# A sparse-attention and gelu kernel: the lead-in of batch 0 and the value rows of batch 1 rearranged

## The chip, the core and the metric

The kernel runs on one core of one Trainium2 chip. The metric is the device time of one execution in microseconds, as the median of several runs.

## What is computed

The input is q, k and v (4 batches, 8 heads, 768 positions, 64 numbers each, float32) and two matrices. Each position attends to its neighbours closer than 16 and, besides, to 24 block keys and block values: the maximum of the keys, and the mean of the values, over blocks of 32. The result goes through two matrix products with a gate between.

```
k_sum = k.reshape(B, H, nb, block, D).max(axis=3)      # block = 32, nb = 24
v_sum = v.reshape(B, H, nb, block, D).mean(axis=3)
scores_l = scale * q @ k^T, kept where |i - j| < 16
scores_s = scale * q @ k_sum^T + log(32)
a = softmax(concat(scores_l, scores_s)); attn = a @ concat(v, v_sum)
x = attn as (3072, 512); h = x @ w_in                  # (512, 2048)
out = (h * sigmoid(1.702 * h)) @ w_out                 # (2048, 512)
```

## The kernel before

The program is one long list of instructions for five engines: TensorE (PE in the profile), VectorE (DVE), ScalarE (ACT), GpSimd (POOL) and SyncE (SP). A small wrapper, `_Ordered`, keeps every instruction in the order in which it is written, so each engine works through its own part of that list in order and waits where an operand isn't ready. All instructions carry line 28, that of the wrapper; the profile's groups are therefore told apart by tile names.

The work goes by batches of 768 positions. Batch 0 is done in two units of 384 positions, unit 0 and unit 1 of the code's `ff_out(u, ...)`: the first half of batch 0, then its second half. Batches 1 to 3 are done whole, with a product in seven parts (`product`) instead of the plain one. For each unit there is an input stage (`ff_in` or `ff_open`: `ph` tiles in PSUM, 128 x 384, four matmuls each, a gelu by ScalarE into `gT`) and an output stage (`ff_out`, twelve slots of four matmuls into `po`). The attention for the next unit is laid between the slots of the output stage by the tables `plan0`, `plan1` and `plan`, and the turning of its keys and queries between the groups of the input stage by the table `todo`. In these tables `s` are scores with an exp by ScalarE, `m` a mask by VectorE, `v` values (`ps_av`, then VectorE's reciprocal and product into `x`), `x` the turning of `x` into `xT`, `t` the turning of queries (`tq`), `R` the value rows (`value_rows`), `g` an early load of the gelu table.

The lead-in is the attention of the first half of batch 0, before any input matmul can run. `load_k0` brings the keys as float32 into `kraw` by DMAs that SP and ScalarE issue; `k_cast` casts them on VectorE into `kb`; `k_turn` turns them on TensorE (`ps_k`), `k_own` copies them into `kn` (shown as `qT`), `k_max` makes the block keys (`ks`), `k_blocks` copies these into `ksz`. Queries, values, `w_in`, the second half's queries and `w_out` come by DMAs that GpSimd issues, which cast on the way. `s_own`, `s_edges` and `b_turn` make the scores to own rows, neighbouring rows and block keys; `v_sum` the block sums of the values (`ps_vt`); `av_own`, `av_edges` and `av_blocks` the values; `v_norm`, `x_turn` and `x_copy` lead to `xT`; `ff_first` is the beginning of the input stage. The mask of the own rows, `near`, and of the edges, `edge`, are added by matmuls with the identity. GpSimd builds them (`masks0`) from tiles that VectorE has filled; the masks of the later stages, `mk`, come from GpSimd in `finish_masks`, which stands ahead of the `w_out` loads.

After the lead-in come, on GpSimd, a copy of rows inside `vw`, the block sums into `vs` (`vrows0`) and the loads of batch 1 (`load_batch(1)`: keys, queries, values); on SP the halo rows (`vw<-vw`) and the sum rows (`vw<-vs`), which the values of unit 0's output stage read.

`value_rows(1)`, the same for batch 1, sums 32 values on TensorE (`vsum`, `ps_vs`), adds on VectorE (`vpart`, `vs`), and lets SP copy the sums into `vw`. It stands in slot 1 of unit 1's output stage; the values that read these rows stand in slot 6.

PSUM is held by two pools for the whole kernel: `pmm`, four tiles of one bank, and `psb`, two tiles of two banks.

Of the kernel before, what the change touches and what calls it, by code (L numbers as in the profile page):

```python
# [35 lines left out]
def kernel(  # L36
# [38 lines left out]
    psb = ctx.enter_context(tc.tile_pool(name="psb", bufs=2, space=bass.MemoryType.PSUM))  # L75
    pmm = ctx.enter_context(tc.tile_pool(name="pmm", bufs=4, space=bass.MemoryType.PSUM))


# [3 lines left out]
    kraw = lead.tile([128, NP, 2, 2, JH * D], F32, name="kraw")  # L82
    kb2, qb2 = {}, {}

    def load_k0(p):
        for e in range(2):
            (act if e else sp).dma_start(out=kraw[:, p, e], in_=k[0, 2 * p:2 * p + 2, e * HALF:(e + 1) * HALF]
                          .rearrange("h (p r) d -> p h (r d)", r=JH))

    def load_q0(half):  # L90
        t = qb2["half", half] = castp2.tile([128, H, JH, D], BF16, name="qb", tag="qb")
        for g in range(2):
            pool.dma_start(out=t[:, 4 * g:4 * g + 4].rearrange("p h r d -> p h (r d)"),
                           in_=q[0, 4 * g:4 * g + 4, half * HALF:(half + 1) * HALF]
                           .rearrange("h (p r) d -> p h (r d)", r=JH))
# [32 lines left out]
    ident = consts.tile([128, 128], BF16, name="ident")  # L128
    E = consts.tile([128, 20 + 128], BF16, name="E")
    warm = lead.tile([128, 512], BF16, name="warm")  # L130
    near = lead.tile([128, JH, 128], BF16, name="near")
    edge = lead.tile([128, NP * JH, 32], BF16, name="edge")
    dve.memset(warm, 0.0)
    dve.memset(E, 0.0)
    sub = E[:, 20:148].rearrange("p (g c) -> p g c", c=block)[:, :, 0:4]
    dve.memset(sub, 1.0)
    dve.memset(near, 0.0)
    dve.memset(edge, FAR)
    dve.memset(edge[0:32], 0.0)
    dve.memset(edge[96:128], 0.0)  # L140
# [5 lines left out]
    def bias(ap, base, pattern, cp):  # L146
        pool.affine_select(out=ap, in_=ap, compare_op=ALU.is_ge, fill=FAR,
                           base=base, pattern=pattern, channel_multiplier=cp)

    def selectors():  # L150
        pool.affine_select(out=sub, in_=sub, compare_op=ALU.is_ge, fill=0.0, base=0,
                           pattern=[[0, 4], [-block, 4]], channel_multiplier=1)
        pool.affine_select(out=sub, in_=sub, compare_op=ALU.is_ge, fill=0.0, base=block - 1,
                           pattern=[[0, 4], [block, 4]], channel_multiplier=-1)

    def masks0():
        reach = window - 1
        bias(near, reach, [[0, JH], [-1, 128]], 1)
        bias(near, reach, [[0, JH], [1, 128]], -1)
        n = NP * JH  # L160
        bias(edge[0:32], reach - 32, [[0, n], [1, 32]], -1)
        bias(edge[96:128], reach - 32, [[0, n], [-1, 32]], 1)
# [32 lines left out]
    ks0 = [keep.tile([128, nb], BF16, name=f"ks0{p}") for p in range(NP)]  # L195
    ksz = lead.tile([128, NP, 64], BF16, name="ksz")
# [15 lines left out]
    def clear_values(eng, s):  # L212
        eng.memset(vw[s][96:128, 0], 0.0)
        eng.memset(vw[s][32:64, NQ - 1], 0.0)
        eng.memset(vw[s][:, :, :, D:VC], 1.0)

    def clear_sums(eng):

        eng.memset(ksz, 0.0)
        eng.memset(vs, 0.0)  # L220
        eng.memset(vs4, 0.0)
# [3 lines left out]
        eng.memset(vs[:, :, D:VC], float(block))  # L225
# [32 lines left out]
    def vsum(s):  # L258

        ps = vs_ps[0] = [pmm.tile([128, 512], F32, name="ps_vs", tag="mm") for e in range(2)]  # L260
# [10 lines left out]
    def warmth(n):  # L271

        for i in range(n):
            ps = pmm.tile([128, 512], F32, name="ps_w", tag="mm")
            pe.matmul(out=ps, lhsT=warm[:, 0:128], rhs=warm, start=True, stop=True)

    def busy(n):
        ps = pmm.tile([128, 512], F32, name="ps_w", tag="mm")
        for i in range(n):
            pe.matmul(out=ps[:, 0:128], lhsT=warm[:, 0:128], rhs=warm[:, 0:128],  # L280
                      start=True, stop=True)
# [87 lines left out]
    def k_cast(p, eng):  # L369
        if p % 2 == 0:  # L370
            kb2[p // 2] = castp2.tile([128, 2, 4, JH, D], BF16, name="kb", tag="kb")
        copy(eng, runs_of(kb2, p).rearrange("p e h r d -> p e h (r d)"), kraw[:, p])

# [7 lines left out]
    def k_turn(p):  # L381
        ps = st["K", p] = pmm.tile([128, 1024], BF16, name="ps_k", tag="mm")
        for e in range(2):
            turn_plain(ps[:, e * HALF:e * HALF + HALF], runs_of(kb2, p)[:, e])
# [5 lines left out]
    def k_max(p):  # L390
        dve.tensor_reduce(out=ks0[p], in_=kn[:, p].rearrange("p (n s) -> p n s", s=block),
                          axis=AX.X, op=ALU.max)

    def k_blocks(p, eng):

        eng.tensor_copy(out=ksz[0:64, p, 0:nb], in_=ks0[p][0:64])
        eng.tensor_copy(out=ksz[64:128, p, 32:32 + nb], in_=ks0[p][64:128])
# [8 lines left out]
    def q_turn(p, half):  # L406
        st["Q", p] = pmm.tile([128, 1024], BF16, name="ps_q", tag="mm")
        turn_plain(st["Q", p][:, 0:HALF], qb2["half", half][:, 2 * p:2 * p + 2])
# [647 lines left out]
```

## Time and profile before

| | |
|---|---|
| median of 3 runs | 229.48 us (228.01 to 229.67) |
| the profiled execution | 229.11 us, of which the span of the profile is 227.1 us |
| TensorE matmul | busy 208.5 us, 92% of the span |
| TensorE weight load | busy 138.4 us, 61% |
| VectorE, ScalarE, GpSimd | busy 132.1, 123.2 and 88.2 us |
| mean granted clock of TensorE | 0.977 |
| software DMA queue (GpSimd) | 12.85 MB, 61456 packets |
| hardware DMA queues | 14.52 and 0.79 MB |
| read from HBM, written | 27.26 and 6.29 MB |

The page divides the span into 40 slices of 5.7 us and gives for each engine a digit, its busy share in tenths; `PEclk` is the clock that TensorE was granted, in tenths. Other answers give busy times for chosen stretches, the waits with what ended them, and the instructions in order of time: start, busy time, engine, operation, out<-in, how many were merged, and in brackets the idle time before with its releaser. "Issue to landing" of a DMA counts from the issue instruction to the arrival of the data. "Start" is in microseconds from the start of the span.

### The profile page before, as it was taken

The numbers are of one execution on the slowest core, as the hardware profiler recorded it, in microseconds if no ns is written. First come the engines' busy times: TensorE is split into PE (matmuls) and PEld (weight loads), VectorE is DVE, ScalarE is ACT, GpSimd is POOL, SyncE is SP. The second block draws the span as 40 slices with busy tenths as digits, with TensorE's granted clock in tenths as the row PEclk, the third lists the DMA queues.
The fourth block names the chain that finished last, engine by engine and source line by source line (L and its number), as shares of the span: only waits on it lengthen the run. The fifth ranks groups of instructions, "written<-read, shape, count | busy, mean of one in ns | idle before, by whom it ended". The sixth has DMA issues, their size and how long they took to land.

```text
span 227.1 us, 5821 instructions
## 1 busy us (share of the span) xinstructions
PE 208.5 (92%) x2354; PEld 138.4 (61%) x2354; DVE 132.1 (58%) x388; ACT 123.2 (54%) x232; POOL 88.2 (39%) x150
## 2 busy tenths in 40 slices
PE   6288899999999869899999999998999999999992
PEld 1245666455555335466578886664788866668882
DVE  6867752559466356479866571698665715543211
ACT  2255478446656614377676354775763547773220
POOL 7998971663359988069448400000000000000000
PEclk9769999999999969999999999999999999999999
DMA  6999999999509999999999957792311680000222
GB/s 190 205 147 196 200 215 219 192 164 189 84 0 92 163 144 151 134 141 148 141 151 156 144 108 213 137 180 38 74 46 49 84 226 16 3 0 0 95 92 94
DMA packets 89146, 28.52 MB, mean 126 GB/s; under 512 B 76816, under 2 KB 86048, under 8 KB 89120
## 3 DMA queue, kind: packets, MB, share of 16 engines
q0 software_dynamic: 61456, 12.85, 68.7%
q1 hardware_dynamic: 26576, 14.52, 29.5%
q10 hardware_dynamic: 1088, 0.79, 1.1%
q8 instruction: 18, 0.29, 0.6%
q14 instruction: 8, 0.07, 0.1%
HBM read 27.26 MB, written 6.29 MB: 148 GB/s over the span
## 4 chain that ended last, share of the span: by engine, by line
PE 65%; DVE 21%; issue 5%; DMA 4%; ACT 2%; SPq 1%; DVEq 0%; ACTq 0%
PE ph L28 23%; PE poA L28 14%; PE po L28 6%; DVE gs L28 6%; PE poB L28 6%; DVE ks L28 4%; PE ps_av L28 4%; PE poC L28 3%; PE ps_s L28 3%; DMA kx<-kb 2%; DVE kx L28 2%; DVE qT L28 2%; PE ps_q L28 2%; DVE x L28 1%; PE ps_t L28 1%
## 5 line engine op out<-in xcount | busy, mean ns | idle before, releaser
L28 PE MATMUL ph<-xT,w_in_sb 128*128 128x384 bf16 x512 | 86.3, 326 | 1.8 <-DVE vpart L28 0.9
L28 ACT ACTIVATE gT<-ph 128x384 f16<-128x384 f32 x128 | 61.4, 491 | 29.7 <-PE ph L28 29.7
L28 PEld LDWEIGHTS <-w_in_sb 128*128 128x128 bf16 x512 | 49.4, 98 | 35.7 <-issue 4.0
L28 PEld LDWEIGHTS <-gT 128*128 128x128 f16 x312 | 29.3, 98 | 11.9 <-issue 0.9
L28 POOL DMA_DIRECT2D vw<-in_v_dram x44 | 31.2, 734 | 10.4 <-DMA vw<-in_v_dram 2.6
L28 DVE TENSOR_TENSOR gs<-gT 128x384 f16<-128x384 f16 x48 | 17.1, 355 | 26.7 <-ACT gT L28 26.6
L28 ACT ACTIVATE a_sb<-ps_s 128x768 bf16<-128x768 f32 x32 | 24.6, 806 | 13.4 <-PE ps_s L28 13.4
L28 PEld LDWEIGHTS <-gs 128*128 128x128 f16 x288 | 27.5, 98 | 3.9 <-issue 0.4
L28 PE MATMUL po<-w_out_sb,gT 128*128 128x512 f16 x96 | 23.9, 390 | 0.0
L28 POOL DMA_DIRECT2D qb<-in_q_dram x24 | 19.3, 832 | 7.9 <-DMA w_out_sb<-in_moe_w_out_dram 3.5
L28 POOL DMA_DIRECT2D kb<-in_k_dram x20 | 16.3, 843 | 8.7 <-DMA kx<-kb 8.6
L28 PE MATMUL poA<-ws,gs 128*128 128x256 f16 x144 | 18.7, 273 | 0.1
L28 DVE TENSOR_TENSOR x<-ps_av,rc 128x384 bf16<-128x384 f32 x32 | 17.8, 558 | 1.1
L28 DVE TENSOR_TENSOR a_sb<-a_sb,mk 128x768 bf16<-128x768 bf16 x28 | 14.6, 553 | 2.6 <-ACT a_sb L28 2.3
L28 ACT ACTIVATE s<-poA 128x256 f32<-128x256 f32 x14 | 5.4, 386 | 18.6 <-PE poA L28 18.3
L28 ACT ACT_TABLE_LOAD x10 | 12.8, 1283 | 3.1 <-issue 2.9
L28 DVE RECIPROCAL rc<-ps_av 128x6 f32<-128x6 f32 x32 | 6.0, 187 | 12.3 <-PE ps_av L28 12.3
L28 DVE TENSOR_TENSOR osb<-poC,s 128x256 f32<-128x256 f32 x9 | 3.8, 421 | 15.9 <-PE poC L28 14.2
L28 PE MATMUL ps_av<-vw,a_sb 128*64 128x65 bf16 (+1 forms) x360 | 9.0, 203 | 2.2 <-DMA vw<-vs 2.2
L28 PEld LDWEIGHTS <-a_sb 128*64 128x64 bf16 (+1 forms) x360 | 7.5, 116 | 5.3 <-issue 4.0
L28 ACT ACTIVATE osb<-po 128x512 f32<-128x512 f32 x6 | 3.6, 598 | 11.8 <-issue 6.2
L28 PEld LDWEIGHTS <-kx 64*128 64x128 bf16 x336 | 6.0, 95 | 5.5 <-issue 3.9
(90 smaller groups left out, 230.0 us busy)
## 6 DMA issues: line engine op xcount, KB each, us to landing
out_dram<-osb SPq DMA_DIRECT2D x24, 256.0 KB, 2.5
vw<-in_v_dram POOLq DMA_DIRECT2D x36, 64.0 KB, 5.9
w_out_sb<-in_moe_w_out_dram POOLq DMA_DIRECT2D x4, 512.0 KB, 12.7
qb<-in_q_dram POOLq DMA_DIRECT2D x8, 192.0 KB, 10.0
w_in_sb<-in_moe_w_in_dram POOLq DMA_DIRECT2D x3, 512.0 KB, 9.8
kb<-in_k_dram POOLq DMA_DIRECT2D x16, 96.0 KB, 5.5
qb<-in_q_dram POOLq DMA_DIRECT2D x16, 96.0 KB, 4.3
vw<-vs SPq DMA_DIRECT2D x6, 198.0 KB, 5.5
```

The lines of the kernel that those rows point to most:

```text
L28: r = f(*a, **kw)
```

## The change

The change has these parts.

- Keys of batch 0: GpSimd issues their loads too, in three DMAs that cast to bfloat16, mixed with the first queries. `kraw` and `k_cast` are gone.
- VectorE's memsets: `clear_keys`, most of `clear_values` and those of `vs` stand after the lead-in.
- Masks: `near` and `edge` are made by VectorE from the identity, by a row of running maxima (`bands`); one edge mask serves all heads. GpSimd makes the identity only. The selector `E` is made by memsets.
- On GpSimd the `w_out` loads stand ahead of `finish_masks`.
- PSUM: the lead-in has three pools of its own (`pidle`, `pturn`, `pbig`), which are closed at its end; `pmm` and `psb` open after it.
- TensorE: ten wide filler matmuls at the start instead of eight, and thirty narrow ones between the first steps (`idle`). The lead-in's order is new: edge scores in two groups, block scores straight from `ks0` by eight matmuls of 32 columns, block sums by matmuls of 32 columns into one tile that a matmul with zeros clears first, copied by one instruction.
- Batch 1: in unit 1's input stage the turns follow each other group by group, all four query turns are there, by `turn_both` with one copy each, and `value_rows(1)` stands behind group 13. In the output stage `plan1` is spread anew; the values of batch 1 draw from `pmm`, the sums (`vsum`) of all batches from `psb`. The last turn of `x` lies between the first input matmuls of batch 1.

```diff
     outp = ctx.enter_context(tc.tile_pool(name="outp", bufs=3))
-    psb = ctx.enter_context(tc.tile_pool(name="psb", bufs=2, space=bass.MemoryType.PSUM))
-    pmm = ctx.enter_context(tc.tile_pool(name="pmm", bufs=4, space=bass.MemoryType.PSUM))
-
-
+    first = ExitStack()
+    pidle = first.enter_context(tc.tile_pool(name="pidle", bufs=2, space=bass.MemoryType.PSUM))
+    pturn = first.enter_context(tc.tile_pool(name="pturn", bufs=2, space=bass.MemoryType.PSUM))
+    pbig = first.enter_context(tc.tile_pool(name="pbig", bufs=2, space=bass.MemoryType.PSUM))
 
     early = ExitStack()
...
-    kraw = lead.tile([128, NP, 2, 2, JH * D], F32, name="kraw")
-    def load_k0(p):
-        for e in range(2):
-            (act if e else sp).dma_start(out=kraw[:, p, e], in_=k[0, 2 * p:2 * p + 2, e * HALF:(e + 1) * HALF]
-                          .rearrange("h (p r) d -> p h (r d)", r=JH))
-
-    def load_q0(half):
-        t = qb2["half", half] = castp2.tile([128, H, JH, D], BF16, name="qb", tag="qb")
-        for g in range(2):
+    def load_k0(p0, p1):
+        for p in range(p0, p1, 2):
+            if p % 2 == 0:
+                kb2[p // 2] = castp2.tile([128, 4, 2, JH, D], BF16, name="kb", tag="kb")
+        o = 2 * (p0 % 2)
+        n = 2 * (p1 - p0)
+        pool.dma_start(out=kb2[p0 // 2][:, o:o + n].rearrange("p h e r d -> p (h e) (r d)"),
+                       in_=k[0, 2 * p0:2 * p1].rearrange("h (e p r) d -> p (h e) (r d)", e=2, r=JH))
+
+    def load_q0(half, gs_):
+        if 0 in gs_:
+            qb2["half", half] = castp2.tile([128, H, JH, D], BF16, name="qb", tag="qb")
+        t = qb2["half", half]
+        for g in gs_:
             pool.dma_start(out=t[:, 4 * g:4 * g + 4].rearrange("p h r d -> p h (r d)"),
...
+    def identity():
+        pool.memset(wide, 0.0)
+        pool.affine_select(out=ident, in_=ident, compare_op=ALU.not_equal, fill=1.0,
+                           base=0, pattern=[[-1, 128]], channel_multiplier=1)
...
-    def masks0():
-        reach = window - 1
-        bias(near, reach, [[0, JH], [-1, 128]], 1)
-        bias(near, reach, [[0, JH], [1, 128]], -1)
-        n = NP * JH
-        bias(edge[0:32], reach - 32, [[0, n], [1, 32]], -1)
-        bias(edge[96:128], reach - 32, [[0, n], [-1, 32]], 1)
+        dve.memset(E, 0.0)
+        for g in range(4):
+            dve.memset(E[32 * g:32 * g + 32, 20 + g:21 + g], 1.0)
+
+    def bands():
+
+        n = 128 + 2 * PAD
+        src, step = wide, 1
+        for dst in (band[0], band[1], band[0], band[1]):
+            n -= step
+            dve.tensor_tensor(out=dst[:, 0:n], in0=src[:, 0:n], in1=src[:, step:step + n], op=ALU.max)
+            src, step = dst, 2 * step
+        n -= 15
+        dve.tensor_tensor(out=band[0][:, 0:n], in0=band[1][:, 0:n], in1=band[1][:, 15:15 + n], op=ALU.max)
+        dve.tensor_scalar(out=band[1][:, 1:1 + n], in0=band[0][:, 0:n], scalar1=-FAR, scalar2=FAR,
+                          op0=ALU.mult, op1=ALU.add)
+        dve.memset(edge, FAR)
+        dve.tensor_copy(out=edge[0:32], in_=band[1][0:32, 2:34])
+        dve.tensor_copy(out=edge[96:128], in_=band[1][96:128, 162:194])
...
     def clear_values(eng, s):
         eng.memset(vw[s][96:128, 0], 0.0)
-        eng.memset(vw[s][32:64, NQ - 1], 0.0)
-        eng.memset(vw[s][:, :, :, D:VC], 1.0)
+        eng.memset(vw[s][96:128, 0, :, D:VC], 1.0)
+        if s:
+            eng.memset(vw[s][32:64, NQ - 1], 0.0)
...
     def vsum(s):
 
-        ps = vs_ps[0] = [pmm.tile([128, 512], F32, name="ps_vs", tag="mm") for e in range(2)]
+        big = psb.tile([128, 1024], F32, name="ps_vs", tag="big")
+        ps = vs_ps[0] = [big[:, 0:512], big[:, 512:1024]]
...
-    def warmth(n):
+    def idle(n, cols=128):
...
+            pe.matmul(out=st["H", 0][:, 0:cols], lhsT=warm[:, 0:128], rhs=warm[:, 0:cols],
                       start=True, stop=True)
...
-    def k_cast(p, eng):
-        if p % 2 == 0:
-            kb2[p // 2] = castp2.tile([128, 2, 4, JH, D], BF16, name="kb", tag="kb")
-        copy(eng, runs_of(kb2, p).rearrange("p e h r d -> p e h (r d)"), kraw[:, p])
...
-    def b_turn(p):
-
-        if p % 2 == 0:
-            st["B", p // 2] = pmm.tile([128, 512], F32, name="ps_b", tag="mm")
-        r = slice(p % 2 * 64, p % 2 * 64 + 64)
-        pe.matmul(out=st["B", p // 2][r, 0:HALF], lhsT=ksz[:, p, :],
-                  rhs=qT[p][0][:, 0:HALF], start=True, stop=True)
+    def e_exp(g):
+        for h in range(2):
+            if g == 0:
+                st["ah", h] = lead.tile([128, HALF], BF16, name="ah", tag=f"ah{h}")
+            o = slice(g * EG, g * EG + EG)
+            act.activation(out=st["ah", h][:, o], in_=st["H", h][:, o], func=ACT.Exp, scale=scale)
+
+    def b_turn(g):
+
+        st["B", g] = pturn.tile([128, 512], F32, name="ps_b", tag="turn")
+        for i in range(2):
+            for h in range(2):
+                o = i * 64 + h * 32
+                r = slice(h * 64, h * 64 + 64)
+                pe.matmul(out=st["B", g][o:o + 32, 0:HALF], lhsT=ks0[r, 2 * g + i],
+                          rhs=qT[2 * g + i][0][r, 0:HALF], start=True, stop=True, skip_group_check=True)
...
-    def v_sum(p):
-
-        if p == 0:
-            st["VT"] = pmm.tile([128, 512], F32, name="ps_vt", tag="mm")
-        r = slice(p % 2 * 64, p % 2 * 64 + 64)
-        for j in range(NJ):
-            o = 20 - 4 * j
-            pe.matmul(out=st["VT"][r, p * 128:p * 128 + 128], lhsT=E[:, o:o + 64],
-                      rhs=vw[0][:, 2 * j + 1, 2 * p:2 * p + 2, 0:D],
-                      start=(j == 0), stop=(j == NJ - 1), skip_group_check=True)
-
-    def v_copy(p, *engs):
-        for hh in range(2):
-            r0 = p % 2 * 64 + hh * 32
-            o = p * 128 + hh * D
-            copy(engs[hh], vs4[r0:r0 + nb, 2 * p + hh, 0:D], st["VT"][r0:r0 + nb, o:o + D])
+    def v_sum(ps_):
+
+        n = len(ps_) * 2 * D
+        p0 = ps_[0]
+        ps = st["VT"] = pturn.tile([128, 512], F32, name="ps_vt", tag="turn")
+        pe.matmul(out=ps[:, 0:n], lhsT=warm[:, 0:128], rhs=warm[:, 0:n], start=True, stop=False,
+                  skip_group_check=True)
+        for p in ps_:
+            for i in range(2):
+                r0, c0 = (p % 2 * 2 + i) * 32, ((p - p0) * 2 + i) * D
+                for j in range(NJ):
+                    o = 20 - 4 * j
+                    pe.matmul(out=ps[r0:r0 + 32, c0:c0 + D], lhsT=E[:, o:o + 32],
+                              rhs=vw[0][:, 2 * j + 1, 2 * p + i, 0:D],
+                              start=False, stop=(j == NJ - 1), skip_group_check=True)
+
+    def v_copy(ps_, eng):
+        n = 2 * len(ps_)
+        copy(eng, vs4[:, 2 * ps_[0]:2 * ps_[0] + n, 0:D],
+             st["VT"][:, 0:n * D].rearrange("p (h d) -> p h d", d=D))
 
...
     def tq(p, s, eng):
-        for half in range(2):
-            ps = pmm.tile([128, 512], F32, name="ps_q", tag="mm")
-            turn_runs(ps[:, 0:HALF], runs_of(qb2, p)[:, half])
-            copy(eng, qT[p][s][:, half * HALF:half * HALF + HALF], ps[:, 0:HALF])
+        ps = turn_both(runs_of(qb2, p))
+        copy(eng, qT[p][s].rearrange("p (e x) -> p e x", e=2), ps)
...
     def values(b, half, g):
 
-        ps = psb.tile([128, 1024], F32, name="ps_av", tag="big")
+        if b == 1:
+            banks = [pmm.tile([128, 512], F32, name="ps_av", tag="mm") for i in range(2)]
+        else:
+            ps = psb.tile([128, 1024], F32, name="ps_av", tag="big")
+            banks = [ps[:, i * 512:i * 512 + 512] for i in range(2)]
...
-    def ff_open(nts):
+    def ff_open(nts, between):
 
         phs = {nt: pmm.tile([128, HALF], F32, name="ph", tag="mm") for nt in nts}
         for kos in ((0, 1), (2, 3)):
             for nt in nts:
                 ff_step(phs[nt], 0, nt, kos)
+            if between and kos[0] == 0:
+                between()
         for nt in nts:
...
-    for p in range(NP):
-        load_k0(p)
+    dve.memset(warm, 0.0)
+    load_k0(0, 1)
     exp_soon()
-    clear_values(dve, 0)
-    clear_sums(dve)
-    for s in range(2):
-        clear_keys(dve, s)
-    clear_values(dve, 1)
-    make_identity(nc, ident)
-    masks0()
-    selectors()
-    load_q0(0)
+    identity()
+    load_k0(1, 2)
+    load_q0(0, (0,))
+    load_k0(2, 4)
+    load_q0(0, (1,))
     for h in range(H):
         load_v0(h)
     for n0, n1 in ((0, 256), (256, 512), (512, 1024), (1024, 1536), (1536, 2048)):
         load_w_in(n0, n1)
     w50 = vw[0].rearrange("p (j e) h c -> p j e h c", e=2)
-    load_q0(1)
-    finish_masks()
+    load_q0(1, (0, 1))
     for c in range(4):
         load_w_out(c)
-    warmth(8)
-    for p in range(NP - 1):
-        k_cast(p, dve)
-        k_turn(p)
-        k_own(p, act)
-        if p:
-            k_max(p - 1)
-    k_cast(3, dve)
+    finish_masks()
+
+    selectors()
+    bands()
+    dve.memset(vw[0][:, :, :, D:VC], 1.0)
+    clear_sums(dve)
+
+    st["H", 0] = pidle.tile([128, 512], F32, name="ps_h", tag="idle")
+    idle(10, 512)
+    k_turn(0)
+    k_own(0, act)
+    idle(8)
+    k_turn(1)
+    k_own(1, act)
+    k_max(0)
+    idle(8)
     q_turn(0, 0)
+    q_turn(1, 0)
     q_copy(0, 0, dve)
-    k_turn(3)
+    q_copy(1, 0, dve)
+    idle(6)
     s_own(0)
-    q_turn(1, 0)
-    q_copy(1, 0, dve)
-    k_own(3, act)
     s_exp(0)
     s_own(1)
     s_exp(1)
-    k_blocks(0, dve)
-    k_blocks(1, dve)
+    k_max(1)
+    idle(4)
+    k_turn(2)
+    k_own(2, act)
+    k_turn(3)
+    k_own(3, dve)
+    idle(4)
+    s_edges(0)
+    e_exp(0)
+    b_turn(0)
+    b_exp(0)
     q_turn(2, 0)
+    q_turn(3, 0)
     q_copy(2, 0, dve)
-    q_turn(3, 0)
     q_copy(3, 0, dve)
+    k_max(2)
     s_own(2)
-    s_edges()
     s_exp(2)
-    e_exp(0)
-    e_exp(1)
-    k_max(2)
-    k_max(3)
-    b_turn(0)
-    b_turn(1)
-    b_exp(0)
-    k_blocks(2, dve)
-    k_blocks(3, dve)
     s_own(3)
     s_exp(3)
-    b_turn(2)
-    b_turn(3)
-    b_exp(1)
-
-    v_sum(0)
-    v_copy(0, dve, dve)
+    v_sum((0, 1))
+    v_copy((0, 1), dve)
+    s_edges(1)
+    e_exp(1)
+    k_max(3)
     av_own(0)
     av_edges(0)
-    v_sum(1)
-    v_copy(1, dve, dve)
+    av_blocks(0)
+    v_sum((2,))
+    v_copy((2,), act)
+    v_norm(0)
     av_own(1)
     av_edges(1)
-    av_blocks(0)
     av_blocks(1)
-    v_norm(0)
+    b_turn(1)
+    b_exp(1)
     v_norm(1)
-    v_sum(2)
-    v_copy(2, act, act)
+    v_sum((3,))
+    v_copy((3,), act)
+    x_turn(0)
     av_own(2)
     av_edges(2)
-    v_sum(3)
-    v_copy(3, dve, dve)
-    av_own(3)
-    av_edges(3)
-    x_turn(0)
+    av_blocks(2)
     x_turn(1)
+    v_norm(2)
     x_copy(0, act)
     x_copy(1, act)
     gelu_soon()
-    av_blocks(2)
+    av_own(3)
+    av_edges(3)
     av_blocks(3)
-    v_norm(2)
     v_norm(3)
     ff_first(0)
     ff_first(1)
     x_turn(2)
+    x_turn(3)
     x_copy(2, dve)
-    x_turn(3)
+    x_copy(3, dve)
     ff_first(2)
-    x_copy(3, dve)
     ff_first(3)
+    first.close()
+    pmm = ctx.enter_context(tc.tile_pool(name="pmm", bufs=4, space=bass.MemoryType.PSUM))
+    psb = ctx.enter_context(tc.tile_pool(name="psb", bufs=2, space=bass.MemoryType.PSUM))
+    clear_values(dve, 0)
+    for s in range(2):
+        clear_keys(dve, s)
     for p in range(NP):
         k_late(p, dve)
         key_halos(p, 0, dve, JH)
-        key_rows(p, 0, ks0[p], dve, JH)
+        key_rows(p, 0, ks0[:, p, 0:nb], dve, JH)
+    dve.memset(vw[1][:, :, :, D:VC], 1.0)
+    clear_values(dve, 1)
+    dve.memset(vs, 0.0)
+    dve.memset(vs[:, :, D:VC], float(block))
     pool.tensor_copy(out=w50[0:64, JH:NJ, 0, :, 0:D], in_=w50[0:64, JH:NJ, 1, :, 0:D])
     vrows0()
     load_batch(1)
...
-    plan1 = {-1: ["s00", "s01", "t2"], 0: ["t3"], 1: ["m00", "m01", "R1"], 2: ["s02", "s03"], 4: ["m02", "m03", "s10", "s11"],
-             6: ["v00", "v01", "m10", "m11"], 7: ["s12", "s13"], 9: ["m12", "m13", "x00", "x01", "g"], 10: ["v10", "v11"], 11: ["x10", "x11"]}
+    plan1 = {-1: ["s00", "s01"], 1: ["m00", "m01"], 2: ["s02", "s03"], 3: ["m02", "m03"], 4: ["s10", "s11"],
+             5: ["m10", "m11"], 6: ["v00", "s12", "s13"], 7: ["v01", "g"], 8: ["m12", "m13"], 9: ["x00", "x01", "v10"],
+             10: ["v11"], 11: ["x10"]}
...
-            7: [lambda: tk(0, 1, dve)], 9: [lambda: tk(1, 1, act)],
-            11: [lambda: tk(2, 1, dve)], 13: [lambda: tk(3, 1, act)], 14: [lambda: tq(0, 1, dve)], 15: [lambda: tq(1, 1, act)]}
+            7: [lambda: tk(0, 1, dve)], 8: [lambda: tk(1, 1, act)], 9: [lambda: tk(2, 1, dve)],
+            10: [lambda: tk(3, 1, act)], 11: [lambda: tq(0, 1, dve)], 12: [lambda: tq(1, 1, act)],
+            13: [lambda: tq(2, 1, dve), lambda: value_rows(1)], 14: [lambda: tq(3, 1, act)]}
...
-                ff_open(order2[0:4])
+                ff_open(order2[0:4], (lambda: tx(1, 1)) if b == 1 else None)
```

## The prediction

> **What bounds the kernel now.** I read the 40 slices of the page first, then the busy times by stretch, then the waits, then the instructions in order of time at the places found.
>
> ```profile
> PE   6288899999999869899999999998999999999992
> PEclk9769999999999969999999999999999999999999
> ```
>
> TensorE is busy nearly everywhere, so time can only be won where a digit is low: the first five slices (to 28 us) and the 14th and 15th (74 to 85 us). The granted clock is low in the same two places.
>
> ```profile
> 0.00:28.00 28.00, 19.78 (x276) 11.36 (x277) 19.82 (x66) 12.39 (x20) 25.65 (x55) 0.88 1.38 188
> 28.00:53.00 25.00, 24.84 (x244) 13.81 (x243) 12.91 (x46) 15.18 (x27) 14.74 (x24) 1.00 1.48 193
> 53.00:93.00 40.00, 35.50 (x470) 20.10 (x469) 24.17 (x50) 20.83 (x36) 26.30 (x45) 0.96 1.25 119
> ```
>
> The columns are stretch, length, busy time of TensorE, its weight loads, VectorE, ScalarE and GpSimd, clock, DMA share and GB/s. TensorE lacks 8.2 us in the lead-in and 4.5 us in unit 1; between them it is full, and so it is after 93.
>
> ```profile
> 5.83 0.97 DVE L28 MEMSET vw<- 32x264 uint32 x3
> 6.72 1.61 DVE L28 CAST kb<-kraw 128x768 bf16<-128x768 f32 x2
> 7.57 0.53 PE L28 MATMUL ps_k<-ident,kb 128*64 128x128 bf16 x12 [2.70 <-DVE kb L28]
> 28.28 9.19 PEld L28 LDWEIGHTS <-w_in_sb 128*128 128x128 bf16 x57 [0.27 <-issue]
> ```
>
> The first key turn waits for VectorE's cast, and the cast stands behind VectorE's memsets, which end at 6.66; the keys had been loading since 0.82 with landings of 3.0 to 5.9 us. TensorE is idle from 4.9 to 7.57, and its clock then is 0.50 from 8.8 to 15.6. The steady matmuls of unit 0's input begin at 28.28.
>
> ```profile
> 76.50 1.90 PE L28 MATMUL po<-w_out_sb,gT 128*128 128x512 f16 x8
> 80.02 0.19 PE L28 MATMUL ps_av<-vw,a_sb 128*64 128x65 bf16 x1 [1.61 <-DMA vw<-vs]
> 80.83 1.50 PE L28 MATMUL ps_av<-vw,a_sb 128*64 128x65 bf16 x47 [0.62 <-DMA vw<-vs]
> 82.26 1.82 PE L28 MATMUL po<-w_out_sb,gT 128*128 128x512 f16 x4
> ...
> 85.52 0.35 PE L28 MATMUL ps_s<-qT,kx 64*128 64x64 bf16 x12 [1.15 <-ACT a_sb L28]
> ...
> 92.71 0.51 PE L28 MATMUL ps_x<-ident,x 128*128 128x128 bf16 x6 [0.88 <-DVE x L28]
> ```
>
> In unit 1 TensorE waits for the block-sum rows, then runs at half clock (80.5 to 83.9), then waits for an exp and for VectorE's normalising.
>
> **Lead-in.** Removed: four casts of 0.87 us and eight ksz copies (2.05 us) on VectorE; most of its opening memsets go behind the lead-in. Added: eleven small VectorE instructions for the masks, which need only the identity (about 2.4 us) and should end near 5, and 30 filler matmuls. The keys' first DMA is now GpSimd's first instruction, at 0.82. Its landing is bounded by 3.0 us (fastest key load of before) and 5.5 us (second query load, same queue, beside other traffic); I take 4.3, since it has the queue alone: 5.1. The ten wide fillers, at 0.43 us each as the eight of before (3.60 us from 1.27), hold TensorE until 5.6, so a landing up to 5.6 costs nothing. From 5.6 TensorE has, at full clock and by rows of before: key turns 4 x 0.55 = 2.2, query turns 1.1, own scores 4 x 0.84 = 3.4, edge scores 0.9, block scores 1.0, block sums 1.6, values 4 x 1.02 = 4.1, x turns 0.7, first input matmuls 1.3, narrow fillers 30 x 0.05 = 1.5: 17.8 us. For waits I follow the order by hand (query copy before the first own scores 0.1, exps 0.2, last normalising and copies 0.6) and add 0.9. Steady matmuls then start at 5.6 + 17.8 + 0.9 = 24.3: **4.0 won**.
>
> Two forms are new. The block scores are eight matmuls of 32 output rows: 0.35 us per four if they share the array as the two of 64 rows did (0.35), 0.65 each group of four if not; 0.5 per group. The block sums are 48 matmuls of 64 columns: 0.0125 us each as in `ps_vs` (48 in 0.60) or 0.08 as in `ps_vt` (6 in 0.49); I take 0.03 plus 0.2 for the three clearing ones. Both ends of all these, with a key landing at 6.3 and with one more stretch of 6.8 us at half clock (up to 3.4 us), give a gain from about -2.7 to +5.5.
>
> Two rules of the Trainium skill speak against this part. "DMA: Bandwidth & Descriptors" (Latency and other measured facts) gives the software path 1 us to the first byte and the hardware path 0.6; its section on the software path's anatomy would land these 393 KB 2.9 us after issue, an estimate by that page, and at 3.7 the fillers would still hide it, so the sum stays. "SBUF — State Buffer" (Who interferes with whom) says that some VectorE copies lock GpSimd out while it writes descriptors; the value loads took 0.85 us each to issue beside VectorE's work and 0.68 to 0.70 later on, which fits it, though the shapes differ; at the later price the sum would differ by nothing on the path.
>
> **GpSimd's queue.** Here the move costs. The built program lets each software DMA wait for the one eight before it to land; the trace shows this wait:
>
> ```profile
> 23.38 3.00 POOL L28 DMA_DIRECT2D w_out_sb<-in_moe_w_out_dram  x4
> 26.42 1.46 POOL L28 COPY vw<-vw 64x1536 bf16<-64x1536 bf16 x1
> ...
> 36.05 0.74 POOL L28 DMA_DIRECT2D qb<-in_q_dram  x1 [2.50 <-DMA w_out_sb<-in_moe_w_out_dram]
> ```
>
> Four key DMAs now stand ahead, and the four `w_out` loads ahead of the masks. The last `w_out` load waits for the third `w_in` load, which landed at 14.4 + 8.0 = 22.4; with the keys ahead of it I take 23.1. Behind it stand the masks (17.95 to 23.38, 5.4 us), the `vw` copy (1.46) and the `vs` copies (1.37): the `vw` copy ends at 30.8 instead of 27.9. Then SP's four halo DMAs (2.68) and two sum DMAs (0.6 each, landing 5.8): the last rows land at 40.0 instead of 37.2. Unit 0's first values need them at 43.11, now 39.1: six us of cover are gone and **0.9 is lost** (0 if they land in 5.0; 3 if the third `w_in` load lands like the fourth, 9.8). The masks themselves (29.3) are needed at 36.7, the last `w_out` chunk (41.2 before) at 46: covered. VectorE's deferred memsets (about 2 us) lie under unit 0's input matmuls; without that cover they would delay the `vs` copies, which wait for the last memset near 30.
>
> **Unit 1.** The stretch 52.5 to 93.05 is 40.55 us. Its work at full clock: input 64 x 0.163 = 10.4, eight turns of 0.78 = 6.2, sums 0.5, scores 8 x 0.23 = 1.9, output 48 x 0.217 = 10.4, values 4 x 0.88 = 3.5, x turns 1.4: 34.3. The other 6.05 are 1.61 + 0.62 (sum rows), 0.6 + 0.95 (47 value matmuls and four output ones at half clock), 1.15 (exp), 0.23 + 0.88 (normalising). Moved: the turns follow each other group by group, all four query turns among them, and the sums stand behind input group 13. Starting at 49.4 they come at 49.4 + 14 x 0.65 + 7 x 0.78 = 64.0; VectorE has a query copy (0.96) and 1.5 of its own ahead, SP issues at 67.0, rows land by 73.1 (5.5). Batch 1's values have landed by 57.5, so nothing earlier waits. The values come in slot 6, at 74.0: 0.9 us of cover. With them the half clock goes. Values now draw from the four-bank pool, so later scores no longer share two buffers with them (1.15); the last x turn lies between input matmuls (0.88). I keep 0.75 for new waits, in the dense turns on VectorE or for banks in slots 7 to 11 (0 to 2): **5.3 won**.
>
> **Later batches.** The sums leave the four-bank pool; the waits of `ph` for `vpart` were 0.17 + 0.75: **0.9 won** (0 to 1.2). Batch 2's loads start earlier with unit 1's turns; its keys landed near 80 and were transposed from 92.3, so they follow.
>
> Sum, from the profiled execution's 229.1 (span 227.1 and 2.0 around it): 229.1 - 4.0 + 0.9 - 5.3 - 0.9 = **219.8**. The median shown, 229.48, is 0.4 higher, less than the spread of its runs.
>
> **Rivals.** (1) The lead-in keeps its length: keys land at 6.3, or the clock halves again. For: its clock was 0.50 for 6.8 us once. Against: the fillers. With 1.0 won: 222.8. (2) Unit 1's wait only changes its name: the sum rows have 0.9 us of cover, and slots 7 and 8 want banks. With 1.0 won instead of 5.3: 224.1. (3) Slower: GpSimd's queue. Every us by which the last `w_out` load waits longer goes through masks, copies, halo and sum DMAs to unit 0's values, one for one. It decides when these rows land after 49.3, 9.3 later than reckoned; at 50.5 the time is 230.3. For: the wait of 2.50 above, and a DMA share above 1 until 55. Against: all `w_in` loads landed by 27.4. (4) The change does not do what it says: what is won is waited for again at batch 1's or 2's loads, which are as long as before: 228.5. Against: the turns need keys that landed by 45.3.
>
> **Chances.** Forecast 0.65 (its own range 216.5 to 222.5), rivals 0.14, 0.08, 0.08, 0.05. A change under 1% (2.3 us) can't be told from none. Faster: 0.65 + 0.14 + 0.08 = 0.87; within 1%: 0.05; slower: 0.08. The range goes from 216, all small waits hidden, to 226, past rivals 1 and 2.
>
> **What would show it.** Right: first `ps_k` near 5.6, clock 1.00 after 6, steady `ph` near 24.3, a wait of `ps_av` for `vw<-vs` near 39 under 2 us, none near 74, the input of batch 1 from about 84.6. Wrong: clock 0.50 after 8, `ph` after 26, a long wait near 39, or idle TensorE between 70 and 84.

## The result, and the profile after

| | before | after |
|---|---|---|
| median | 229.13 us (228.01 to 229.67, 4 runs) | 220.33 us (219.63 to 221.68, 4 runs) |
| profiled execution, its span | 229.11, 227.1 us | 220.85, 218.9 us |

The ratio is 0.9629 (95% interval 0.9565 to 0.9693): 8.8 us, or 3.7%, are won. The forecast was 219.8 us, between 216 and 226. Executions come in a faster and a slower state, and a ratio compares runs of the faster one alone; of the changed kernels below only `e3_lead_only` had slower runs, two of its ten, and its median and range include them.

The 40 slices of the page of after, TensorE and the clock:

```profile
PE   7969999499999999999999999999999989999993
PEclk9999999999999999999999999999999999999999
```

The low digits of the lead-in are down to two, and those of slices 14 and 15 are gone. But there is a 4 in slice 8 (38 to 44 us) where before had a 9: something new, and it is the dearest thing that the change left behind. The busy times of the stretches that the prediction read (length, TensorE, weight loads, VectorE, ScalarE, GpSimd, clock, DMA share, GB/s) say the same:

```profile
0.00:28.00 28.00, 24.29 (x361) 15.03 (x362) 17.01 (x67) 14.13 (x27) 20.86 (x36) 1.00 1.33 145
28.00:53.00 25.00, 22.04 (x226) 12.25 (x225) 12.54 (x40) 13.12 (x22) 17.10 (x36) 1.00 1.49 202
53.00:93.00 40.00, 39.98 (x508) 23.12 (x507) 25.01 (x52) 25.07 (x44) 28.76 (x49) 1.00 1.44 139
```

TensorE was idle for 8.2, 0.2 and 4.5 us in these stretches; now it is idle for 3.7, 3.0 and nothing. Where the two traces part is best read from the starts of four stages. "Steady" is the first input matmul after which the input stage of unit 0 runs on without a break; the other columns are the first `po` of unit 0's output stage, the first `ph` of unit 1 and the first `ph` of batch 1. The later rows are the experiments below, all from their profiled executions.

```
               steady   output, unit 0   input, unit 1   input, batch 1   span
before          27.75        39.55           52.48           93.05        227.1
after           24.50        36.18           52.09           86.25        218.9
e1_q_one        24.64        36.31           49.84           84.00        216.4
e2_masks_first  24.57        36.25           49.41           83.56        216.6
e3_lead_only    24.16        35.84           53.23           92.64        225.4
e4_unit1_only   27.74        39.55           52.47           86.63        219.8
e5_keys_split   23.82        35.50           48.59           82.75        215.4
e6_no_fill      26.68        38.35           51.41           85.57        217.5
e7_rows_late    24.86        36.54           49.49           88.32        221.0
e8_vsum_pmm     24.64        36.32           49.56           83.72        217.6
e9_joined       23.65        35.32           48.24           82.40        215.3
```

By differences of before and after: the lead-in wins 3.37, the output stage of unit 0 loses 2.98 (it lasts 15.91 instead of 12.93), unit 1 wins 6.41 (34.16 instead of 40.57), the rest wins 1.40. The sum is 8.2, the difference of the spans. One turn of `x` (0.33) has moved from unit 1 to behind the next start, so that by work unit 1 wins 6.1 and the rest 1.7.

The lead-in of after, in order of time on TensorE:

```profile
5.68 0.85 PE L28 MATMUL ps_k<-wide,kb 128*64 128x128 bf16 x12
12.50 0.86 PE L28 MATMUL ps_k<-wide,kb 128*64 128x128 bf16 x24 [1.52 <-DMA kb<-in_k_dram]
24.50 1.78 PE L28 MATMUL ph<-xT,w_in_sb 128*128 128x384 bf16 x10 [0.45 <-DVE xT L28]
```

The first key turn follows the wide fillers at once, where before waited for a cast. New is the wait at 12.50 for the keys of pairs 2 and 3. The first line also shows half speed: twelve turns in 0.85 us, against 0.53 for twelve at full speed.

GpSimd's queue and the end of its path, the values of unit 0:

```profile
12.74 0.82 POOL L28 DMA_DIRECT2D vw<-in_v_dram  x1 [1.84 <-DMA kb<-in_k_dram]
25.62 0.74 POOL L28 DMA_DIRECT2D w_out_sb<-in_moe_w_out_dram  x1 [3.24 <-DMA w_in_sb<-in_moe_w_in_dram]
26.36 0.22 POOL L28 MEMSET mk<- 128x128 bf16 x1
32.00 1.46 POOL L28 COPY vw<-vw 64x1536 bf16<-64x1536 bf16 x1
36.25 1.23 SPq L28 DMA_DIRECT2D vw<-vs  x2
42.00 0.19 PE L28 MATMUL ps_av<-vw,a_sb 128*64 128x65 bf16 x1 [2.20 <-DMA vw<-vs]
42.76 0.54 PE L28 MATMUL ps_av<-vw,a_sb 128*64 128x65 bf16 x23 [0.57 <-DMA vw<-vs]
```

Read from the bottom: TensorE waits 2.77 us in two pieces for rows that SP issues at 36.25, because the `vw` copy ends at 33.41, because the masks ahead of it begin only at 26.36, because the fourth `w_out` load was held for 3.24 us by a `w_in` load. And the value load at 12.74 is held by the 384 KB key load, 8.1 us from issue to landing.

Unit 1 of after:

```profile
67.36 0.60 PE L28 MATMUL ps_vs<-vw,E 64*32 64x128 bf16 x48
78.14 0.57 PE L28 MATMUL ps_av<-vw,a_sb 128*64 128x65 bf16 x24
86.25 1.46 PE L28 MATMUL ph<-xT,w_in_sb 128*128 128x384 bf16 x8
```

None of these has a bracket: the block sums run in the input stage, and the values 10.8 us later wait for nothing.

### The profile page after: what moved, and what is told of

Same layout as the page of the kernel before. It is cut to its first block, busy times and chain, and to the rows that moved or that the text cites. A ratio compares the mean times of both kernels' runs of the same rounds, so it can differ in the third digit from the quotient of the medians.

```text
span 218.9 us, 5916 instructions
## 1 busy us (share of the span) xinstructions
PE 207.7 (95%) x2419; PEld 139.7 (64%) x2419; DVE 127.3 (58%) x378; ACT 123.1 (56%) x233; POOL 88.6 (40%) x147
## 2 busy tenths in 40 slices
DMA packets 89066, 27.74 MB, mean 127 GB/s; under 512 B 78784, under 2 KB 85968, under 8 KB 89040
## 4 chain that ended last, share of the span: by engine, by line
PE 75%; DMA 13%; POOL 6%; DVE 2%; issue 1%; SPq 1%; ACT 1%; POOLq 0%
PE ph L28 32%; PE poA L28 14%; PE po L28 8%; PE poB L28 6%; DMA w_in_sb<-in_moe_w_in_dram 4%; DMA kb<-in_k_dram 4%; PE poC L28 4%; PE ps_av L28 3%; PE ps_t L28 3%; DMA vw<-vs 3%; PE ps_s L28 2%; POOL mk L28 2%; DMA xT<-x 2%; SPq L28 1%; POOL vw L28 1%
## 5 line engine op out<-in xcount | busy, mean ns | idle before, releaser
L28 PE MATMUL po<-w_out_sb,gT 128*128 128x512 f16 x96 | 22.8, 380 | 0.0
L28 POOL DMA_DIRECT2D kb<-in_k_dram x23 | 19.3, 862 | 6.8 <-DMA kx<-kb 5.9
L28 PE MATMUL poA<-ws,gs 128*128 128x256 f16 x144 | 18.7, 273 | 0.1
L28 DVE TENSOR_TENSOR x<-ps_av,rc 128x384 bf16<-128x384 f32 x32 | 17.8, 558 | 1.1
L28 PE MATMUL poA<-w_out_sb,gT 128*128 128x256 f16 x72 | 9.4, 273 | 0.0
L28 PE MATMUL poB<-w_out_sb,gs 128*128 128x256 f16 x72 | 9.4, 273 | 0.0
## 6 DMA issues: line engine op xcount, KB each, us to landing
w_out_sb<-in_moe_w_out_dram POOLq DMA_DIRECT2D x4, 512.0 KB, 17.4
```

The lines of the kernel that those rows point to most:

```text
L28: r = f(*a, **kw)
```

## The experiments

**Does GpSimd stand behind a landing, and what is that worth?** Two kernels take the wait on `w_out` away by different means. The first keeps the order and makes one DMA fewer:

```diff
-    load_q0(1, (0, 1))
+    t1 = qb2["half", 1] = castp2.tile([128, H, JH, D], BF16, name="qb", tag="qb")
+    pool.dma_start(out=t1.rearrange("p h r d -> p h (r d)"),
+                   in_=q[0, :, HALF:S].rearrange("h (p r) d -> p h (r d)", r=JH))
```

> The changed kernel with one edit: the two loads of the second half's queries are one load, so one software DMA fewer stands ahead of the last w_out load. Theory 1 (GpSimd stands behind the landing of the DMA eight before): the last w_out load then waits for the second w_in load instead of the third, which landed near 25.5; it issues near 21.7, the masks begin near 22.5, the vw copy ends near 29.5 instead of 33.5, the last sum rows land near 38, and the 2.8 us that TensorE waits near 40 for vw<-vs go: 217.6. Theory 2 (the rows are late because 16 full DMA engines are slow to land them, whatever GpSimd does): the wait stays over 2 us, 220.3.

Measured: 218.15 us (217.33 to 218.41), ratio 0.9541 [0.9491, 0.9592].

```profile
22.55 0.74 POOL L28 DMA_DIRECT2D w_out_sb<-in_moe_w_out_dram  x1 [0.17 <-issue]
32.52 1.26 POOL L28 COPY vs<-vs 24x128 bf16<-24x128 bf16 x4 [2.06 <-DVE vs L28]
40.51 0.54 PE L28 MATMUL ps_av<-vw,a_sb 128*64 128x65 bf16 x23 [0.41 <-DMA vw<-vs]
```

With one DMA fewer in front, the last `w_out` load stands, by the count of eight, behind the second `w_in` load instead of the third, and its 3.24 us become 0.17. The next thing that is late shows in the second line: the `vs` copies wait for VectorE's clearing of `vs`, one of the memsets that the change put behind the lead-in. Of the 2.77 us on TensorE 0.41 are left.

The second leaves the number of DMAs and moves the masks:

```diff
+    finish_masks()
     for c in range(4):
         load_w_out(c)
-    finish_masks()
```

> The changed kernel with finish_masks ahead of the w_out loads, as it stood before. Theory 1: masks from 19.8 to 25.2, w_out issued by 28.2, vw copy ended near 29.7, last sum rows landed near 38.2, no wait near 40: 217.6. Theory 2: wait as before the edit, 220.3. Theory 3 (the w_out loads come 5.5 us later and land later): the wait for the sum rows goes, but TensorE waits for w_out instead at 36 or in the output stage: 219 to 222.

Measured: 217.83 us (217.39 to 218.42), ratio 0.9527 [0.9471, 0.9584]. The masks now run while the `w_in` loads land; the `w_out` loads follow at 25.98 with no wait, and no wait is listed for the values of unit 0 either, though the 24 take 0.81 us where an undisturbed group takes 0.57:

```profile
25.98 2.99 POOL L28 DMA_DIRECT2D w_out_sb<-in_moe_w_out_dram  x4
29.02 1.46 POOL L28 COPY vw<-vw 64x1536 bf16<-64x1536 bf16 x1
39.80 0.81 PE L28 MATMUL ps_av<-vw,a_sb 128*64 128x65 bf16 x24
```

So theory 1 holds by two routes. The wait is for the landing of the DMA eight before, and it goes one for one through masks and copy to SP's DMAs: in e1 the masks, the `vw` copy and the halo DMAs all come 3.0 to 3.1 us earlier. It costs about 2.5 us (220.33 to 217.83). The intervals of the ratios still overlap a little with that of the changed kernel, but no run of e1 or e2 is as slow as its fastest. The later landing of `w_out` cost nothing: TensorE waits for none of these loads.

**Do the two parts of the change add up?** One kernel has the lead-in alone, with unit 1, the pools' use by values and sums, and the later batches as before:

```diff
-    plan1 = {-1: ["s00", "s01"], 1: ["m00", "m01"], 2: ["s02", "s03"], 3: ["m02", "m03"], 4: ["s10", "s11"],
+    plan1 = {-1: ["s00", "s01", "t2"], 0: ["t3"], 1: ["m00", "m01", "R1"], 2: ["s02", "s03"], 4: ["m02", "m03", "s10", "s11"],
...
-                ff_open(order2[0:4], (lambda: tx(1, 1)) if b == 1 else None)
+                ff_open(order2[0:4])
```

> The changed kernel with its second part undone: tables plan1 and todo, tq, the pools of values and vsum and the last x turn as before. Theory 1 (the parts add up): unit 1 again takes 40.5 us instead of 34.2 and the later batches 1.4 more, while the lead-in's 3.4 are nearly all eaten by the 2.8 of waiting for sum rows near 40: 228.1, that is no more than 1 below the kernel before. Rival (the lead-in's gain is needed for unit 1's or the other way round): 224 to 226, with unit 1 shorter than 39.

Measured: 227.43 us (224.99 to 231.73, 10 runs), ratio 0.9929 [0.9886, 0.9972].

```profile
41.34 0.19 PE L28 MATMUL ps_av<-vw,a_sb 128*64 128x65 bf16 x1 [1.88 <-DMA vw<-vs]
42.23 0.54 PE L28 MATMUL ps_av<-vw,a_sb 128*64 128x65 bf16 x23 [0.69 <-DMA vw<-vs]
42.98 3.26 PE L28 MATMUL po<-w_out_sb,gT 128*128 128x512 f16 x8
```

By the start of unit 0's output the lead-in has won 3.7 us, and this output stage gives 4.5 back: 2.6 in the two waits, the rest at half clock behind them (eight output matmuls take 3.26 us, 1.90 in after). At unit 1's input this kernel is 0.75 us *later* than before. What this execution has gained by the end comes from elsewhere: unit 1 is 1.2 shorter, where TensorE did not fall to half clock this time, and the rest 1.3, of which 0.60 are waits for `xT<-x` that before has and this execution has not, and 0.56 lie behind the last matmuls. As it was made, the new lead-in was spent before unit 1 began, and the whole kernel was 0.7% faster.

The other has the second part alone, on the lead-in of before.

> The kernel before with only the second part of the change: value rows and all turns in unit 1's input stage, the new plan1, the values of batch 1 in pmm, vsum in psb, the last x turn between input matmuls. Lead-in and GpSimd's order as before. Theory 1 (the parts add up): no half clock and no wait near 75, 6.4 from unit 1 and 1.4 from later batches: 221.4. Rival (the part needs the lead-in's earlier start of loads): 223 to 226, with a wait for vw<-vs left in unit 1.

Measured: 221.98 us (221.48 to 222.35), ratio 0.9714 [0.9664, 0.9763]. Unit 1 lasts 34.16 us, to the hundredth as in after. So 7.1 us of the 8.8 are the second part's; with the 1.6 of the lead-in alone the parts add to 8.7, each of these known to about 1 us by its interval.

**What sets the lead-in's length now?** Built on e2: the keys of pairs 2 and 3 come in two loads instead of one.

```diff
-    load_k0(2, 4)
+    load_k0(2, 3)
+    load_k0(3, 4)
     load_q0(0, (1,))
```

> The kernel of e2 (masks ahead of the w_out loads; it took 217.8 us against 229.05 before), with the one 384 KB load of key pairs 2 and 3 made two loads of 192 KB; nothing is left out. In e2 TensorE waits 1.40 us at 12.5 for that load, which takes 8.1 us from issue, where loads of half its size took 3.6 to 4.5. Theory A (the size of the one load makes it late): the two land by 10.5, the wait is gone, time 216.4 (216.0 to 217.0). Theory B (the bytes of keys, queries and values share one rate until about 12): the last key lands near 12.5 as before, time 217.8 (217.4 to 218.2). Theory C (the extra load costs GpSimd 0.8 us that comes back as a wait for sum rows near 40): up to 218.6.

Measured: 217.1 us (216.88 to 218.69), ratio 0.9488 [0.9436, 0.9539].

```profile
10.71 0.53 PE L28 MATMUL ps_k<-wide,kb 128*64 128x128 bf16 x12
12.15 0.53 PE L28 MATMUL ps_k<-wide,kb 128*64 128x128 bf16 x12 [0.91 <-DMA kb<-in_k_dram]
```

Pair 2 is there in time; pair 3 is turned at 12.15, when in e2 both were turned from 12.53. The last keys are thus usable only 0.4 us earlier, although their load is half as large: the two loads took 6.0 and 7.0 us from issue to landing, where the first key load took 3.6. So mostly they wait for what shares the queue with them (theory B); whether that is the bytes ahead of them or those issued behind them was not separated. Another 0.4 comes from pair 2's turn, which no longer stands behind the wait, so that theory A's 1.4 us come to 0.75 at the steady start. In the whole time this is 0.7 us, less than the intervals of e2 and e5 tell apart. Theory C's wait near 40 did not appear.

Built on e2 as well: without the thirty narrow fillers.

```diff
-    idle(8)
...
-    idle(6)
...
-    idle(4)
```

> The kernel of e2 (217.8 us) without the 30 narrow filler matmuls of the lead-in; the ten wide ones at the start stay. Theory A (the fillers keep the granted clock up): the clock falls to about half somewhere between 6 and 15 us, and the 10 us of TensorE work behind the key wait stretch, so that the steady input matmuls start 1 to 3 us later: 219 to 221. Theory B (up to 12.5 us the lead-in waits for landings anyway): the fillers ahead of the key wait are free, only the last four, 0.2 us, are won: 217.6 (217.2 to 218.0).

Measured: 218.26 us (217.58 to 219.29), ratio 0.9513 [0.9464, 0.9563], the same as e2 within the intervals. Its trace is not the same. The stretch from 10 to 16 us (columns as above) and the two marks on TensorE:

```profile
10.00:16.00 6.00, 4.40 (x72) 2.73 (x70) 1.80 (x2) 3.35 (x6) 3.67 (x6) 0.50 2.08 157
```

```profile
12.83 1.49 PE L28 MATMUL ps_k<-wide,kb 128*64 128x128 bf16 x24 [1.57 <-DMA kb<-in_k_dram]
26.68 9.91 PE L28 MATMUL ph<-xT,w_in_sb 128*128 128x384 bf16 x60 [0.45 <-DVE xT L28]
```

The clock is 0.50, twenty-four turns take 1.49 us instead of 0.86, and the steady matmuls start 2.1 us later than in e2, as theory A said. The 2.1 is still there at batch 1's input (85.57 against 83.56), but only 0.9 is left in the spans: in the last batch TensorE of e2 waits 1.11 us for `xT<-x`, and in this kernel it does not. The fillers are worth 2.1 us of lead-in; in these executions 1.1 of that is waited away at the end, and the whole times (0.4 us apart) don't show that anything is left of it.

**Which piece of unit 1's part wins?** Built on e2: the value rows go back to slot 1 of the output stage; pools, turns and slots stay as in after.

```diff
-            13: [lambda: tq(2, 1, dve), lambda: value_rows(1)], 14: ...
+            13: [lambda: tq(2, 1, dve)], 14: ...
-    plan1 = {-1: ["s00", "s01"], 1: ["m00", "m01"], ...
+    plan1 = {-1: ["s00", "s01"], 1: ["R", "m00", "m01"], ...
```

> The kernel of e2 (217.8 us), with batch 1's value rows put back from unit 1's input stage (behind group 13) to slot 1 of its output stage, where before.py had them; pools, the dense turns and the new spread of slots stay. Theory A (most of unit 1's gain is the early start of the sum rows): the sums run near 70.5, the rows land near 79, and the values near 75.5 wait 2 to 3.5 us for them, with a stretch at half clock behind that: 220.3 to 222.3. Theory B (the gain is from the pools, the turns and the spread): the rows land in time or nearly so, 218.0 to 218.8.

Measured: 221.48 us (220.3 to 222.93), ratio 0.9667 [0.9599, 0.9734].

```profile
77.63 0.19 PE L28 MATMUL ps_av<-vw,a_sb 128*64 128x65 bf16 x1 [0.89 <-DMA vw<-vs]
78.70 0.54 PE L28 MATMUL ps_av<-vw,a_sb 128*64 128x65 bf16 x23 [0.88 <-DMA vw<-vs]
79.63 1.52 PE L28 MATMUL po<-w_out_sb,gT 128*128 128x512 f16 x4
```

In the profiled execution unit 1 lasts 38.83 us instead of 34.15: 4.7 of its gain of 6.4 are the early start of the sums. 1.8 of these are the two waits; the half clock behind them (four `po` in 1.52 us, 1.04 in e2; the mean clock from 78 to 85 us is 0.76) makes about 7 x 0.24 = 1.7, and 1.0 are two small waits around the sums themselves. Theory A. But the profile is of the slowest of four runs. Two of them, with a mean clock of 0.99, took 222.5 and 222.9 us, and the other two, with 1.00, 220.3 and 220.4: this fits a half clock that came in some executions only, and the medians of e7 and e2 are 3.7 us apart, not 4.7.

Built on e2, for the later batches: the sums draw from the four-bank pool again.

```diff
-        big = psb.tile([128, 1024], F32, name="ps_vs", tag="big")
-        ps = vs_ps[0] = [big[:, 0:512], big[:, 512:1024]]
+        ps = vs_ps[0] = [pmm.tile([128, 512], F32, name="ps_vs", tag="mm") for e in range(2)]
```

> The kernel of e2 (217.8 us), with the block sums of all batches drawing their two banks from the four-bank pool again, as in before.py. Theory A (the prediction's term for the later batches): waits of ph for vpart of about 0.9 us in all come back, 218.7 (218.4 to 219.0). Theory B (the gain of 1.4 us in the later batches comes from the last turn of x and other things): under 0.4 us, 217.8 to 218.2.

Measured: 219.49 us (219.38 to 219.87), ratio 0.9580 [0.9540, 0.9620]. The list of waits has again, as two pieces of 0.17 and 0.79 us:

```profile
PE ph L28 <- DVE vpart L28: 1.0, 2, 0.8
```

That is the wait of theory A, to a tenth. The whole time rose by 1.7, to above theory A's range, and the span by 1.0; the intervals of the two ratios overlap, so the wait is shown by the trace and its price only roughly by the times.

**Joined.** On e5, one query load as in e1, and the clearing of `vs` ahead of the late key copies:

```diff
+    dve.memset(vs, 0.0)
+    dve.memset(vs[:, :, D:VC], float(block))
     clear_values(dve, 0)
...
     clear_values(dve, 1)
-    dve.memset(vs, 0.0)
-    dve.memset(vs[:, :, D:VC], float(block))
```

> The kernel of e5 (masks ahead of the w_out loads, keys of pairs 2 and 3 in two loads; 217.1 us), with the two second-half query loads made one, as in e1, and VectorE's clearing of vs moved ahead of the late key copies, where it no longer holds GpSimd's sum copies for 2.06 us. Nothing is left out. Theory A (what was moved off GpSimd's queue now lies beside TensorE's work, and no value matmul of unit 0 waits any more): no further gain, 217.1 (216.6 to 217.6), with the sum copies some 2 us earlier and no wait near 39. Theory B (the queue still sets something on the path, such as batch 1's or batch 2's loads): 215.5 to 216.4.

Measured: 216.8 us (216.13 to 217.82), ratio 0.9510 [0.9478, 0.9542]. The `vs` copies run at 28.55, 2.8 us earlier than in e5, and the time is that of e5 within the intervals: theory A. This kernel and e5 are the fastest; the interval lies below that of after, and it is 1.2 hundredths of before's time faster.

## Why the prediction was right, and where it was off

The time, 219.8, came out at 220.33, by the mechanisms named; that it came so close is partly luck. Against the sum, GpSimd's queue lost 1.9 us more and the lead-in won 0.6 less, while unit 1 won 1.1 more and the later batches 0.5 more. By spans the sum forecast 217.8 and 218.9 was found.

*Lead-in, 4.0 reckoned, 3.4 found.* The first key turn (5.6) is at 5.68, the steady start (24.3) at 24.50. The step that failed is the row it was measured from: the prediction took a weight load at 28.28 of before, while the `ph` that stands in the same place of the program starts at 27.75; that is 0.5 of the 0.6. Inside the sum errors of both signs cancel. The keys of pairs 2 and 3 were not looked at as a landing at all, only the first one was, and TensorE waited 1.52 us for them, which makes 2.2 us of waits in all instead of 0.9; the fillers took 2.4 us in place of 1.5, the first eight of them still at half speed, and the block sums with their clearing 1.9 in place of 1.6. Against that the values took 3.1 (4.1 reckoned), the own scores 2.9 (3.4), the first input matmuls 0.7 (1.3, the work of eight, of which four lie behind the steady start) and the block scores 0.8 (1.0), each from its start to the next one's. Part of this is how the sum was made: it took busy times, and a busy time runs on past the start of the next instruction. Own scores are 0.50 + 0.34 = 0.84 so, but in the same profile of before 0.43 + 0.28 from start to start. The first key load took 3.6 us (4.3 reckoned) and the fillers hid it. From the first key turn to the steady start 18.8 us passed, 18.7 were reckoned.

*GpSimd's queue, 0.9 lost reckoned, 2.8 found.* This is the term that was mis-sized, with the right chain. The third `w_in` load was put at 23.1 and landed near 25.6, when the load that waited for it was issued. The value loads ahead of it were held 1.84 us by the big key load, and the `w_in` loads were issued from 14.57 instead of 12.82. So the third was issued 1.75 us later than in before, and then took 9.3 us to land instead of 8.0; the prediction had put 0.7 for both. Why it took 1.3 longer was not separated. Every later step follows with that 2.5: the `vw` copy ended at 33.4 instead of 30.8, the last rows landed near 42.8 instead of 40.0. The bound of 3 held. The two missed waits, TensorE's at 12.50 and GpSimd's at 12.74, are for one and the same transfer.

*Unit 1, 5.3 reckoned, 6.4 found.* Of the 0.75 kept for new waits nothing was needed. The schedule was reckoned well: SP issues the sum rows 17.8 us after the start of the unit's input (17.6 reckoned); the values come 26.1 us after it (24.6 reckoned), which left more cover still. That the early rows with the clock behind them are the larger part (4.7 in the profiled executions), e7 shows; of the other 1.7, 0.33 are the moved turn of `x`, and the shares of pools and spread were not separated.

*Later batches, 0.9 reckoned, 1.4 found.* e8 shows the 0.9. Besides, 0.54 are won behind the last matmuls (5.18 us from the start of the last eight to the end of the span, now 4.64), 0.33 are lost to the moved turn of `x` and 0.2 to longer waits for `xT<-x`, which differ between 0 and 1.1 us in these profiles; 0.5 of gain is left that I can't assign.

*The rivals.* The queue, the slower case, has the true place: it decided 2.8 us, not 9.3. The lead-in did not keep its length, unit 1's wait did not change its name (no bracket at 78.14), and what was won was not waited for at batch 1's loads.

## What to carry to other kernels

When loads are put at the head of a queue, follow the landing of every one of them, not of the first alone, and then the instructions of the same engine that wait for those landings: here one key load made TensorE wait 1.52 us, and GpSimd's wait for a weight load eight DMAs ahead another 2.8. Work that needs no transfer (the masks, 5.4 us) belongs in front of an instruction that will have to wait, not behind it: the same instructions in the other order were worth 2.5 us. And a wait of TensorE has two prices, its own length and the half clock that may follow; in the profiled execution of e7 they were as large as each other.

## What the runs showed of the hardware

- The clock column can miss a half clock. In the profile of e4 it is 1.00 throughout the lead-in, and yet twelve key turns take 0.85 us and two `near` matmuls 0.82, as in before where the column says 0.50 (0.53 and 0.50 at full speed). In after, too, it is 1.00 while the first twelve turns take 0.85 us. Durations of a known instruction are the safer reading, but it must be the same one: the turns of unit 1, which show the same shape, take 0.85 us in both kernels beside input matmuls at full speed (four in 0.82).
- Half clock is not always paid. In e4 the matmuls are slow until about 17 us, in before until 15.6, and the steady start is 27.74 and 27.75: both reach the same `ps_s` matmuls at 17.4, in before behind a wait of 0.50 us for VectorE. In the new lead-in, where TensorE sets it, half clock costs 2.1 us (e6).
- After waits of the same kind and nearly the same length the clock fell in some executions and not in others: behind 2.57 us in two pieces at 42 us in e3 it did, behind 2.77 us in after it did not; behind 2.23 us at 80 us in before it did, behind 2.38 in e3 it did not. What decides it stays open. The Trainium skill ("TensorE: Matmul & The Clock Gate", "HAM oscillation — how this bites in real kernels") gives as a rule that TensorE shall have no idle gaps over about 3.4 us; here waits of 0.89 and 0.88 us, 1.1 us apart, were followed by half clock in e7, so shorter gaps can be enough.
- A software DMA of 384 KB took 8.1 us, where 192 KB took 3.6 to 4.5 early in the queue; the two of 192 KB in its place (e5) took 6.0 and 7.0, and the second was usable only 0.4 us earlier. Here, then, what shares the queue counts more than the size of one load.
